# First expert of the second mixture: identity products in TensorE's waits, no zeroed output, Sinkhorn's sums in PSUM, one plain pair, another order of steps

## The chip, the cores and the metric

The kernel runs on one core of one Trainium2 chip, in fp32 throughout. The metric is device time in microseconds from launch to end, the median of three executions. TensorE runs at one of two granted clock levels, 1.2 or 2.4 GHz; a granted clock of 0.50 in a row is the lower one and 1.00 the upper. Engines are written here as TensorE (PE in the profile, PEld its weight loads), VectorE (DVE), ScalarE (ACT), GpSimd (POOL), and SP, which issues the DMAs.

## The reference

An attention stage (two kinds of softmax attention, added) gives `x` of 2304 tokens x 512. A soft mixture of 8 experts follows, and then the second mixture, in which the change lies:

```python
def _moe2_ref(x, w_gate, w1, w2):
    N, D = x.shape
    E = w_gate.shape[1]                       # 8 experts, D 512, F 1024, N 2304
    logits = x @ w_gate
    P = np.exp(logits - logits.max())
    for _ in range(8):                        # Sinkhorn
        P /= P.sum(1, keepdims=True) + 1e-09  # row sums
        P /= P.sum(0, keepdims=True) + 1e-09  # column sums
        P *= N / E
    out = np.zeros((N, D), dtype=np.float32)
    for e in range(E):
        h = np.maximum(x @ w1[e], 0.0)
        out += P[:, e:e + 1] * (h @ w2[e])
    return out
```

## The kernel before

The first mixture ends with a product `so` (L881) of eight experts' second weights, each half expert waiting for its own DMA of 1 MB. Its result goes through two copies (L888 on VectorE, L889 on ScalarE), a small product `sop` (L892) and a copy to `soT` (L895). x itself is never formed: `x = c @ slot_out`, so the second mixture folds `slot_out` into its first weights. `a_part` (L937 and the two engines' copies) and `a_sum` (L948, L952, L953) make this folded weight `a4s` for one half of an expert's 1024 hidden units.

The second mixture then takes 8 experts by 9 blocks of 256 tokens. In each block, `z_mm` (L1008) makes the hidden units z1 and z0 (two halves) in PSUM. ScalarE applies the ReLU and rounds to the fast matmul type (the high part, L1020, L1041), VectorE or GpSimd makes the low part (L1024, L1045), so that three fast products stand for one fp32 product. VectorE's `z_sum` (L1035) adds or subtracts quarters of h. The 2x2 product h @ w2 is computed by Strassen's scheme with seven products instead of eight: `product` (L1066, 12 matmuls each), from weight tiles `wt` whose high part ScalarE writes (`w_hi`, L991) and whose low part VectorE or GpSimd writes (`w_lo`, L998). Four of the weight tiles are sums of quarters of w2 (`w_sum`, L978, the tiles `ts`). The first block of the first expert is done plainly, with eight products (`plain`, L1079, 96 matmuls), since it needs no sums. Each block adds into `acc` by five updates (L1100, up_a to up_e), which VectorE reads from PSUM.

While the first expert runs, the gates are made beside it: `gate` (logits, their maximum, exp), then eight rounds of `sink`, each with row sums (L1182 to L1185), a matmul with ones for the column sums over partitions (L1189) and the column division (L1196 to L1200). A generator's step of these runs after each fifth product. The first expert adds without its gate, and is scaled by it later (L1143).

The order of all this is written by a table of numbers: each step is put on a plan `at(t, f, ...)`, where t is in units of one product, and the plan is sorted and issued. `P` holds the places of a block's steps, `W` those of the weight steps of experts 1 to 7 (with 0 or 1 for VectorE or GpSimd), `W0` and `P0` those of the first expert's weights and its plain block. Each engine does its own instructions in that order and waits at each for what it needs. PSUM has four buffers of one bank for y, ap, as, gl, gp and sp together, and two banks each for z1 and z0.

## Time and profile before

| what | us |
|---|---|
| median of 3 executions | 1060.66 (1058.97 to 1060.85) |
| the profiled execution, its own time | 1060.58 |
| its span, first to last instruction | 1058.9 |
| TensorE busy | 994.4 (94%) |
| VectorE busy | 744.3 (70%) |
| GpSimd busy | 642.8 (61%) |
| ScalarE busy | 546.2 (52%) |

So 1.7 us of the execution lie outside the span. Up to about 209 us the attention and the first mixture run. The first expert of the second mixture runs from there to about 361 us, and experts 1 to 7 to the end. Shares over the whole span hide that the stages differ, so the rows below are taken by stretch.

### The profile page before, as it was taken

The page shows a single profiled execution, that of the slowest core. Times are in us where ns is not written, and L with a number is a line of the kernel's source. Part 1 is how long each engine was busy: PE and PEld are TensorE (multiplying, and loading weights), DVE is VectorE, ACT ScalarE, POOL GpSimd, SP SyncE. Part 2 cuts the span into 40 slices and gives each one's busy share as a digit, 9 for nine tenths or more (in the row PEclk, how much of TensorE's full clock was granted, in tenths as well). Part 3 has the DMA queues.
Part 4 walks back from the last instruction along what each step waited for, and adds up shares of the span by engine and source line. Part 5 has one row for each costly group of instructions (what it writes and reads, how often), then busy time and mean ns, then how long its engine had stood idle before and what let it go on. Part 6 is the DMA issues. An engine that isn't in the chain of part 4 may idle for free.

```text
span 1058.9 us, 23713 instructions
## 1 busy us (share of the span) xinstructions
PE 994.4 (94%) x9663; PEld 919.1 (87%) x9663; DVE 744.3 (70%) x1264; ACT 546.2 (52%) x1032; POOL 642.8 (61%) x497
## 2 busy tenths in 40 slices
PE   6898888869887999999999999999999999999998
PEld 6777763249787989999999999999989999999998
DVE  4878762276889767686677767767767686677766
ACT  4666641143433655665555456545644564456543
POOL 5777552055355746784767486657746874768453
PEclk9999898869999999999999999999999999999999
DMA  9999999924001110130013001301120130000111
GB/s 192 175 187 238 261 312 391 387 79 157 1 1 41 60 62 2 41 120 1 1 41 120 2 2 39 120 1 41 53 68 2 41 98 23 2 2 21 40 61 61
DMA packets 86593, 93.89 MB, mean 89 GB/s; under 512 B 52052, under 2 KB 52052, under 8 KB 86484
## 3 DMA queue, kind: packets, MB, share of 16 engines
q1 hardware_dynamic: 86484, 92.37, 31.3%
q8 instruction: 77, 1.26, 0.6%
q14 instruction: 32, 0.26, 0.1%
HBM read 87.64 MB, written 4.72 MB: 87 GB/s over the span
## 4 chain that ended last, share of the span: by engine, by line
PE 55%; POOL 1%; DVE 0%; issue 0%
PE y L1066 49%; PE z L1008 5%; PE ap L937 1%; POOL wt L998 1%; PE as L948 0%; DVE acc L1100 0%
## 5 line engine op out<-in xcount | busy, mean ns | idle before, releaser
L1066 PE MATMUL y<-wt,ot 128*128 128x256 f32 x5964 | 770.0, 280 | 15.2 <-DVE acc L1100 9.5
L1066 PEld LDWEIGHTS y<-wt,ot 128*128 128x128 f32 x5964 | 737.1, 189 | 32.1 <-issue 19.4
L1045 POOL TENSOR_TENSOR ot<-ft,ot 128x512 fp32r<-128x512 f32 x284 | 379.1, 1356 | 296.8 <-ACT ot L1041 218.9
L1100 DVE SCALAR_TENSOR_TENSOR acc<-y,pg,acc 128x256 f32<-128x256 f32 x315 | 201.4, 639 | 186.1 <-PE y L1066 185.4
L1041 ACT ACTIVATE ot<-ft 128x512 fp32r<-128x512 f32 x284 | 172.4, 628 | 179.2 <-DVE ft L1035 179.1
L1020 ACT ACTIVATE ot<-z 128x512 fp32r<-128x512 f32 x217 | 129.3, 597 | 184.1 <-PE z L1008 149.8
L1035 DVE SCALAR_TENSOR_TENSOR ft<-z,ft 128x512 f32<-128x512 f32 x284 | 193.3, 681 | 0.2
L1008 PE MATMUL z<-c,a4s 128*128 128x256 f32 x576 | 160.7, 281 | 3.3 <-DVE ft L1035 2.4
L1024 DVE SCALAR_TENSOR_TENSOR ot<-z,ot 128x512 fp32r<-128x512 f32 x217 | 147.6, 681 | 0.0
L1008 PEld LDWEIGHTS z<-c,a4s 128*128 128x128 f32 x576 | 109.0, 190 | 4.6 <-DVE ft L1035 3.5
L1031 ACT ACTIVATE ft<-z 128x512 f32<-128x512 f32 x142 | 84.1, 592 | 0.0
L998 POOL TENSOR_TENSOR wt<-w2s,wt 128x1024 fp32r<-128x1024 f32 x16 | 38.6, 2410 | 10.0 <-ACT wt L991 10.0
L998 POOL TENSOR_TENSOR wt<-ts,wt 128x1024 fp32r<-128x1024 f32 x16 | 39.1, 2461 | 0.0
L509 POOL TENSOR_TENSOR pl<-pl,l 128x384 f32<-128x384 f32 x16 | 13.3, 832 | 40.5 <-DVE l L505 25.6
L520 DVE STREAM_TRANSPOSE bd<-pl 32x384 f32<-32x384 f32 x64 | 36.4, 569 | 1.4
L991 ACT ACTIVATE wt<-ts 128x1024 fp32r<-128x1024 f32 x32 | 33.6, 1054 | 6.6 <-DVE ts L978 3.3
L1100 DVE SCALAR_TENSOR_TENSOR acc<-y,acc 128x512 f32<-128x512 f32 (+1 forms) x44 | 24.6, 562 | 17.2 <-PE y L1066 11.9
L978 POOL TENSOR_TENSOR ts<-w2s 128x1024 f32<-128x1024 f32 x14 | 33.6, 2402 | 0.0
L399 ACT ACTIVATE kt<-knt 64x576 f32<-64x576 f32 x32 | 20.6, 644 | 14.1 <-DVE kd L391 13.8
L391 DVE TENSOR_REDUCE kd<-knt 128x144 f32<-128x576 f32 x16 | 12.1, 757 | 19.9 <-PE knt L341 13.7
L991 ACT ACTIVATE wt<-w2s 128x1024 fp32r<-128x1024 f32 x25 | 26.0, 1049 | 0.0
L998 DVE TENSOR_TENSOR wt<-ts,wt 128x1024 fp32r<-128x1024 f32 x16 | 25.1, 1568 | 0.0
(179 smaller groups left out, 852.2 us busy)
## 6 DMA issues: line engine op xcount, KB each, us to landing
wa<-in_moe_w_dram SPq DMA_DIRECT2D x32, 1024.0 KB, 12.6
w1s<-in_moe_w_dram SPq DMA_DIRECT2D x16, 1024.0 KB, 5.1
w2s<-in_moe_w_dram SPq DMA_DIRECT2D x16, 1024.0 KB
vw<-in_v_dram SPq DMA_DIRECT2D x62, 96.0 KB, 6.0
...
```

The lines of the kernel that those rows point to most:

```text
L520: nc.vector.transpose(out=bds[u % 2][32 * c:32 * c + 32, :, c, :], in_=U[u]["pl"][32 * c:32 * c + 32])
L991: nc.scalar.activation(out=tt[e, i][:, 0], in_=w_of(e, i), func=ACTF.Copy)
L998: eng.tensor_tensor(out=t[:, 1], in0=w_of(e, i), in1=t[:, 0].bitcast(FP32), op=ALU.subtract)
L1008: nc.tensor.matmul(out=zt[n, k][:, f, :], lhsT=a4s[e % 2][:, f0:f0 + 128], rhs=c4[:, BLK * b:BLK * b + BLK], start=True, stop=True,)
L1020: nc.scalar.activation(out=t[:, 0], in_=zv(n, i, k), func=ACTF.Relu)
L1024: nc.vector.scalar_tensor_tensor(out=t[:, 1], in0=zv(n, i, k), scalar=0.0, in1=t[:, 0].bitcast(FP32), op0=ALU.max, op1=ALU.subtract)
L1031: nc.scalar.activation(out=t, in_=zv(n, i, k), func=ACTF.Relu)
L1035: nc.vector.scalar_tensor_tensor(out=t, in0=zv(n, i, k), scalar=0.0, in1=ft[n, other], op0=ALU.max, op1=op)
L1041: nc.scalar.activation(out=t[:, 0], in_=ft[n, name], func=ACTF.Copy)
L1045: nc.gpsimd.tensor_tensor(out=t[:, 1], in0=ft[n, name], in1=t[:, 0].bitcast(FP32), op=ALU.subtract)
L1066: nc.tensor.matmul(out=yt[n, bank][:, HD * half:HD * half + HD], lhsT=ot[n, name][:, l, f, :], rhs=tt[e, j][:, r, f, :], start=(m == 0 and ...
L1100: nc.vector.scalar_tensor_tensor(out=o, in0=in_, scalar=pg[:, t, e:e + 1] if e else 1.0, in1=o, op0=ALU.mult, op1=ALU.add)
```

## The change

Six edits, all but the last in the first expert or just before it:

1. `fill(n)` issues n identity products (128x128 times 128x128, into a PSUM tile that nothing reads): 9 before each half of the last two experts' `so`, 3 before `sop`, 4 after it, 4 after the first `a_part` and 4 after the first `a_sum`.
2. `acc` is no longer zeroed by GpSimd (five memsets, L1296). The first update of each part of `acc` is a copy. `CP = (1, 0)`: for the first 128 tokens of a block it is done by ScalarE, for the second by VectorE. `up_b` of the first expert becomes a ScalarE copy of one half and a VectorE addition of the other.
3. Sinkhorn's row sums and column sums lie in the PSUM tile `sp` instead of SBUF, taken at the start of a round instead of at its matmul, and the last two instructions (divide, times N/E) become one.
4. `gate_part`'s copy of `soT` (L1217) goes from VectorE to ScalarE.
5. The first expert's weights are loaded in the order w1 half 1, w2 half 1, w1 half 0, w2 half 0, and the second `a_part`/`a_sum` are steps of the plan.
6. New tables: `P1` for the first expert's blocks (P stays for the others), and new numbers in `P0`, `W0` and `W`.

```diff
+P1 = {'z1': 5.13,
+ 'z0': 3.41,
...
+CP = (1, 0)
+FILL = (9, 3, 4, 4, 4)
...
- '6l': (67.58, 1),
- 'ld1': 9.4,
- 'ld2': 9.71}
+ '6l': (67.81, 0),
+ 'ld1': 2.33,
+ 'ld2': 16.73}
...
+        idle = ps.tile([128, 512], FP32, name="idle", tag="idle", bufs=1)
+
+        def fill(n):
+            for _ in range(n):
+                nc.tensor.matmul(out=idle[:, 0:128], lhsT=ident, rhs=ident, start=True, stop=True)
...
+                if e >= E - 2 and j % 4 == 0:
+                    fill(FILL[0])
                 nc.tensor.matmul(
                     out=so[32 * g:32 * g + 32, :], lhsT=hT[:, j, e, :], rhs=w[:, j % 4, :],
...
-        if not e:
-            need(("zero", t // 4))
         o = acc[:, t, :] if out_ is None else acc[:, t, HD * out_:HD * out_ + HD]
         if in_.shape != o.shape:
             o = o.rearrange("p (h d) -> p h d", h=2)
+        if first and not e:
+            if CP[i]:
+                nc.scalar.activation(out=o, in_=in_, func=ACTF.Copy)
+            else:
+                nc.vector.tensor_copy(out=o, in_=in_)
+            return
         nc.vector.scalar_tensor_tensor(
...
     def up_b(n):
-        update(n, 0, None, yt[n, 0])
+        if n < NB:
+            update(n, 0, 1, yt[n, 0][:, HD:], True)
+            update(n, 0, 0, yt[n, 0][:, 0:HD])
+        else:
+            update(n, 0, None, yt[n, 0])
...
     def sink():
-        nc.vector.tensor_reduce(out=rs[:, :, 0], in_=pg, axis=AX.X, op=ALU.add)
+        sp = yt.tile("sp", [128, DM], FP32, "sp", "y")
+        rs = sp[:, 160:160 + NT]
+        cs = sp[:, 192:192 + E]
+        nc.vector.tensor_reduce(out=rs, in_=pg, axis=AX.X, op=ALU.add)
         nc.vector.tensor_scalar(out=rs, in0=rs, scalar1=EPS, scalar2=None, op0=ALU.add)
         nc.vector.reciprocal(out=rs, in_=rs)
...
-        nc.vector.tensor_tensor(out=pg, in0=pg, in1=cs_.to_broadcast([128, NT, E]), op=ALU.mult)
-        nc.vector.tensor_scalar(out=pg, in0=pg, scalar1=float(N) / E, scalar2=None, op0=ALU.mult)
+        nc.vector.scalar_tensor_tensor(
+            out=pg, in0=pg, scalar=float(N) / E,
+            in1=cs.rearrange("p (o e) -> p o e", o=1).to_broadcast([128, NT, E]), op0=ALU.mult, op1=ALU.mult,
+        )
...
-    for i in range(2):
+    for i in (1, 0):
         load_w1(0, i)
-    for i in (1, 0):
         load_w2(0, i)
...
+    a_part(0, 1)
+    fill(FILL[3])
+    a_sum(0, 1)
+    fill(FILL[4])
...
-        nc.vector.tensor_copy(out=so4, in_=soT.to_broadcast([128, KD, 4, NS]))
+        nc.scalar.activation(out=so4, in_=soT.to_broadcast([128, KD, 4, NS]), func=ACTF.Copy)
```

Three places where the order moves. The first is TensorE from the last half expert of `so` to the first products of the plain block; before, its rows are these (ap, as: the folded weight of one half; z1, z0: hidden units; y: products):

```order
L881 MATMUL so_2898<-wa_2843,hT_2882 32x512 x4
L892 MATMUL sop_3007<-stack_70,hs_2884 128x32 x4
L937 MATMUL ap_3064<-w1s_3050,soT_77 32x512 x4
L937 MATMUL ap_3072<-w1s_3048,soT_77 32x512 x4
L948 MATMUL as_3080<-aps_3069,a4s_3024 128x512 x2
L948 MATMUL as_3085<-aps_3077,a4s_3024 128x512 x2
L1008 MATMUL z1_3098<-c4_2885,a4s_3024 128x256 x4
L1008 MATMUL z0_3106<-c4_2885,a4s_3024 128x256 x4
L1079 MATMUL y_3120<-wt_3057,ot_3103 128x256 x12
```

And after (idle: the identity products):

```order
L842 MATMUL idle_2762<-ident_69 128x128 x9
L924 MATMUL so_2899<-wa_2844,hT_2883 32x512 x4
L842 MATMUL idle_2762<-ident_69 128x128 x3
L936 MATMUL sop_3047<-stack_70,hs_2885 128x32 x4
L842 MATMUL idle_2762<-ident_69 128x128 x4
L982 MATMUL ap_3107<-w1s_3090,soT_77 32x512 x4
L1272 MATMUL idle_3106<-ident_69 128x128 x4
L993 MATMUL as_3119<-aps_3112,a4s_3068 128x512 x2
L1272 MATMUL idle_3106<-ident_69 128x128 x4
L982 MATMUL ap_3133<-w1s_3094,soT_77 32x512 x4
L1053 MATMUL z1_3142<-c4_2886,a4s_3068 128x256 x4
L993 MATMUL as_3151<-aps_3138,a4s_3068 128x512 x2
```

The second half's `a_part` and `a_sum` stand behind the first half's, around z1, and the identity products fill the places between.

The second is VectorE in the first expert's third and fourth blocks, where one round of Sinkhorn ends and the next begins (pg: the gates; rs, cs: row and column sums). Before:

```order
L953 TENSOR_TENSOR a4s_3024<-as_3640,a4s_3024 64x512
L1196 TENSOR_REDUCE cs_3047<-sp_3625 128x8
L1197 TENSOR_SCALAR cs_3047<-cs_3047 128x8
L1198 RECIPROCAL cs_3047<-cs_3047 128x8
L1199 TENSOR_TENSOR pg_76<-pg_76,cs_3047 128x144
L1200 TENSOR_SCALAR pg_76<-pg_76 128x144
L1100 SCALAR_TENSOR_TENSOR acc_3023<-y_3623,acc_3023 128x256
L1182 TENSOR_REDUCE rs_3046<-pg_76 128x18
L1183 TENSOR_SCALAR rs_3046<-rs_3046 128x18
L1184 RECIPROCAL rs_3046<-rs_3046 128x18
L1185 TENSOR_TENSOR pg_76<-pg_76,rs_3046 128x144
```

And after, at the same round:

```order
L998 TENSOR_TENSOR a4s_3068<-as_3682,a4s_3068 64x512
L1250 TENSOR_REDUCE sp_3611<-sp_3611 128x8
L1253 TENSOR_SCALAR sp_3611<-sp_3611 128x8
L1254 RECIPROCAL sp_3611<-sp_3611 128x8
L1255 SCALAR_TENSOR_TENSOR pg_76<-pg_76,sp_3611 128x144
L998 TENSOR_TENSOR a4s_3068<-as_3724,a4s_3068 64x512
L1236 TENSOR_REDUCE sp_3736<-pg_76 128x18
L1237 TENSOR_SCALAR sp_3736<-sp_3736 128x18
L1238 RECIPROCAL sp_3736<-sp_3736 128x18
L1239 TENSOR_TENSOR pg_76<-pg_76,sp_3736 128x144
L1149 SCALAR_TENSOR_TENSOR acc_3067<-y_3666,acc_3067 128x256
```

Every instruction of a round now has an operand in the PSUM tile sp, L1200 is gone, and the update of acc that stood between the two rounds stands behind both.

The third is GpSimd in the first expert's weights (ts: sums of w2's quarters, wt: low parts). Before:

```order
L1296 MEMSET acc_3023 128x2048
L998 TENSOR_TENSOR wt_3063<-w2s_3052,wt_3063 128x1024
L978 TENSOR_TENSOR ts_3093<-ts_3093,w2s_3052 128x1024
L978 TENSOR_TENSOR ts_3128<-w2s_3052,ts_3093 128x1024
L1296 MEMSET acc_3023 128x2048
L998 TENSOR_TENSOR wt_3056<-w2s_3054,wt_3056 128x1024
L1296 MEMSET acc_3023 128x2048
L998 TENSOR_TENSOR wt_3059<-ts_3128,wt_3059 128x1024
```

And after:

```order
L1023 TENSOR_TENSOR ts_3128<-ts_3128,w2s_3092 128x1024
L1043 TENSOR_TENSOR wt_3105<-w2s_3092,wt_3105 128x1024
L1023 TENSOR_TENSOR ts_3223<-w2s_3092,ts_3128 128x1024
L1043 TENSOR_TENSOR wt_3098<-w2s_3096,wt_3098 128x1024
L1043 TENSOR_TENSOR wt_3101<-ts_3223,wt_3101 128x1024
L1043 TENSOR_TENSOR wt_3102<-ts_3128,wt_3102 128x1024
```

The memsets are gone, and the second sum (`ts`) stands ahead of the first low part.

## Rows read from the trace of the kernel before

**Rows 1.** The page's first part: busy us, share, instructions of each engine.

```profile
PE 994.4 (94%) x9663; PEld 919.1 (87%) x9663; DVE 744.3 (70%) x1264; ACT 546.2 (52%) x1032; POOL 642.8 (61%) x497
```

**Rows 2.** TensorE's waits, 207 to 360 us, then (last row) from 360: us, times, longest.

```profile
PE y L1066 <- DVE acc L1100: 9.5, 5, 3.9
PE z L1008 <- DVE ft L1035: 2.4, 2, 1.6
...
PE y L1066 <- POOL wt L998: 3.8, 4, 1.2
```

**Rows 3.** Stretches: length, busy of PE, PEld, DVE, ACT, POOL, granted clock, DMA, GB/s.

```profile
252.60:364.70 112.10, 98.35 (x774) 93.47 (x774) 95.75 (x177) 48.49 (x82) 56.24 (x38) 0.95 0.03 11
...
206.00:208.00 2.00, 1.23 (x12) 0.20 (x8) 0.00 (x0) 0.00 (x0) 0.00 (x0) 0.50 1.05 388
```

**Rows 4.** TensorE's instructions by line, 252.6 to 364.7 us: count, busy, mean ns, idle before.

```profile
L1066 PE MATMUL y<-wt,ot 128*128 128x256 f32 x671 | 94.3, 289 | 11.1 <-DVE acc L1100 9.5 <-DVE ot L1024 1.5
L1008 PE MATMUL z<-c,a4s 128*128 128x256 f32 x64 | 18.6, 291 | 2.6 <-DVE ft L1035 2.4
```

**Rows 5.** TensorE's timeline in a later expert: start, us, instructions.

```profile
515.21 6.06 PE L1066 MATMUL y<-wt,ot 128*128 128x256 f32 x52
521.11 0.28 PE L1008 MATMUL z<-c,a4s 128*128 128x256 f32 x1
```

**Rows 6.** VectorE's instructions by line, 252.6 to 364.7 us.

```profile
L1100 DVE SCALAR_TENSOR_TENSOR acc<-y,acc 128x512 f32<-128x512 f32 (+1 forms) x39 | 22.6, 580 | 11.9 <-PE y L1066 11.8
...
L1199 DVE TENSOR_TENSOR pg<-pg,cs 128x144 f32<-128x144 f32 x8 | 8.6, 1069 | 0.3
L1200 DVE TENSOR_SCALAR pg<-pg 128x144 f32<-128x144 f32 x8 | 6.7, 834 | 0.3
L1185 DVE TENSOR_TENSOR pg<-pg,rs 128x144 f32<-128x144 f32 x8 | 5.0, 621 | 0.3
L1183 DVE TENSOR_SCALAR rs<-rs 128x18 f32<-128x18 f32 x8 | 4.8, 600 | 0.3
```

**Rows 7.** Timeline of VectorE and GpSimd around 280 us.

```profile
277.52 0.69 DVE L953 TENSOR_TENSOR a4s<-as,a4s 64x512 fp32r<-64x512 f32 x1
279.82 2.17 DVE L1199 TENSOR_TENSOR pg<-pg,cs 128x144 f32<-128x144 f32 x1
...
279.48 2.35 POOL L978 TENSOR_TENSOR ts<-w2s 128x1024 f32<-128x1024 f32 x1
```

**Rows 8.** TensorE's timeline from the last experts of `so` to the second block.

```profile
200.47 1.06 PE L881 MATMUL so<-wa,hT 128*32 128x512 f32 x8
207.66 1.93 PE L881 MATMUL so<-wa,hT 128*32 128x512 f32 x8 [0.78 <-DMA wa<-in_moe_w_dram]
210.24 1.89 PE L892 MATMUL sop<-stack,hs 128*128 128x32 f32 x8 [0.64 <-DVE hs L888]
...
213.18 3.64 PE L937 MATMUL ap<-w1s,soT 128*32 128x512 f32 x16 [1.05 <-DMA w1s<-in_moe_w_dram]
219.38 1.62 PE L1008 MATMUL z<-c,a4s 128*128 128x256 f32 x8 [0.54 <-DVE a4s L953]
225.76 4.61 PE L1079 MATMUL y<-wt,ot 128*128 128x256 f32 x26 [2.31 <-DVE ot L1024]
232.89 1.06 PE L1220 MATMUL gp<-wg_sb,so 128*128 128x8 f32 x8 [2.52 <-DVE so L1217]
...
247.07 0.62 PE L1066 MATMUL y<-wt,ot 128*128 128x256 f32 x4
```

**Rows 9.** Weight loads around one Sinkhorn product (two passes of 144 columns).

```profile
263.62 0.30 PEld L1189 LDWEIGHTS sp<-pg,a4s 128*128 128x128 f32 x2
263.85 0.89 PEld L1066 LDWEIGHTS y<-wt,ot 128*128 128x128 f32 x7
```

**Rows 10.** VectorE's timeline: the copy for the gates' product.

```profile
229.69 3.15 DVE L1217 COPY so<-soT 128x512 f32<-128x512 f32 x1
```

**Rows 11.** Low parts of weights on VectorE, whole span: ns min/median/max.

```profile
L998 DVE TENSOR_TENSOR wt<-ts,wt x16: 1226/1346/2867, 236.5 to 965.2; 128x1024 fp32r<-128x1024 f32 x16
```

More of the change, by code (lines that the diff above doesn't have):

```diff
@@ L77 @@
  'ue': 7.47}
-NPLAIN = 1
-P0 = ((-3.45, -3.16, -2.01, 1.77, -1.6, 2.91, -0.95, 0.59, 5.1, 6.1, 8.71, 8.08),
- (-1.58, 2.82, -3.83, -10.07, -3.18, 3.82, 1.07, -4.42, 1.7, 2.01, 10.07, 9.98))
-W0 = {'0h': -9.21,
- '6h': -6.84,
- '1h': -4.85,
- '7h': -0.9,
- '2h': 2.44,
- '3h': 2.25,
- '4h': 3.75,
- '5h': 4.98,
- 'gp': 2.21,
- 'g': 4.46,
- '0l': (-8.05, 0),
- '6l': (-5.5, 1),
- '1l': (-2.28, 0),
- '7l': (1.08, 1),
- 't1': (-7.68, 0),
- 't2': (-0.28, 1),
- 't4': (0.56, 1),
- 't3': (3.48, 0),
- '2l': (2.5, 1),
- '3l': (5.33, 0),
- '4l': (4.74, 0),
- '5l': (5.44, 1)}
-W = {'ap': 14.61,
- 'as': 19.65,
- 't1': (22.65, 1),
- 't2': (33.72, 1),
- 't4': (38.68, 1),
- 't3': (40.91, 1),
- '0h': 44.89,
- '1h': 41.33,
- '2h': 57.7,
- '3h': 59.91,
- '4h': 56.58,
- '5h': 61.69,
- '6h': 66.19,
- '0l': (48.68, 1),
- '1l': (45.62, 0),
- '2l': (59.61, 1),
- '3l': (62.44, 1),
- '4l': (59.48, 0),
- '5l': (65.8, 0),
- '6l': (67.58, 1),
- 'ld1': 9.4,
- 'ld2': 9.71}
+P1 = {'z1': 5.13,
+ 'z0': 3.41,
+ 'a12h': -3.58,
+ 'a12l': -1.99,
+ 'h22': -4.08,
+ 'a11h': -1.57,
+ 's1': -1.49,
+ 'h11': -2.05,
+ 'a11l': -1.4,
+ 'a22h': -0.77,
+ 's2': -1.31,
+ 'a22l': -0.67,
+ 's2h': 0.14,
+ 's2l': 0.89,
+ 's4': -0.35,
+ 's1h': -0.3,
+ 's3': 0.49,
+ 's1l': 0.04,
+ 's3h': 2.53,
+ 's3l': 3.57,
+ 's4h': 2.73,
+ 's4l': 4.29,
+ 'ua': 2.0,
+ 'ub': 4.76,
+ 'ud': 5.16,
+ 'uc': 5.93,
+ 'ue': 7.23}
+NPLAIN = 1
+CP = (1, 0)
+FILL = (9, 3, 4, 4, 4)
+P0 = ((-4.08, -3.79, -3.03, 0.91, -0.28, 3.53, 1.09, 1.8, 6.07, 7.22, 7.12, 10.0),
+ (-4.0, 6.94, -19.64, -11.36, 2.38, -1.13, 12.86, -14.23, 7.99, -0.51, 3.32, 12.21))
+W0 = {'ap': -8.9,
+ 'as': -3.41,
+ '0h': -12.47,
+ '6h': -10.55,
+ '1h': -3.76,
+ '7h': 2.78,
+ '2h': 3.51,
+ '3h': 5.6,
+ '4h': 6.66,
+ '5h': 5.66,
+ 'gp': 2.2,
+ 'g': 3.57,
+ '0l': (-9.11, 0),
+ '6l': (-3.19, 1),
+ '1l': (-2.75, 0),
+ '7l': (3.45, 1),
+ 't1': (-24.54, 0),
+ 't2': (-5.8, 1),
+ 't4': (3.1, 1),
+ 't3': (4.64, 0),
+ '2l': (5.77, 1),
+ '3l': (6.91, 1),
+ '4l': (8.5, 0),
+ '5l': (7.12, 0)}
+W = {'ap': 14.93,
+ 'as': 21.66,
+ 't1': (27.31, 1),
+ 't2': (34.27, 1),
+ 't4': (38.09, 1),
+ 't3': (41.61, 1),
+ '0h': 50.43,
+ '1h': 42.64,
+ '2h': 56.78,
+ '3h': 59.79,
+ '4h': 56.6,
+ '5h': 61.35,
+ '6h': 65.61,
+ '0l': (53.1, 0),
+ '1l': (48.5, 1),
+ '2l': (60.79, 1),
+ '3l': (61.41, 1),
+ '4l': (59.9, 0),
+ '5l': (66.97, 0),
+ '6l': (67.81, 0),
+ 'ld1': 2.33,
+ 'ld2': 16.73}
 class Ring:
@@ L1146, in attn_moe_moe_kernel @@
     nc.gpsimd.memset(ones, 1.0)
-    rs = mm.tile([128, NT, 1], FP32, name="rs")
-    cs_ = mm.tile([128, 1, E], FP32, name="cs")
     def gate():
@@ L1209, in attn_moe_moe_kernel, with fill @@
         tt.tile((0, i), [128, 2, HF, HD], FP32R, "wt", "t")
-    for i in (1, 0):
-        a_part(0, i)
-    for i in (1, 0):
-        a_sum(0, i)
+    zt.tile("idle", [128, HF, BLK], FP32, "idle", "z0")
+    def fill(n):
+        for _ in range(n):
+            nc.tensor.matmul(out=zt["idle"][:, 0, 0:128], lhsT=ident, rhs=ident, start=True, stop=True)
+    a_part(0, 1)
+    fill(FILL[3])
+    a_sum(0, 1)
+    fill(FILL[4])
     def gate_part():
         so4 = ft.tile("so4", [128, KD, 4, NS], FP32, "so4", "f")
-        nc.vector.tensor_copy(out=so4, in_=soT.to_broadcast([128, KD, 4, NS]))
+        nc.scalar.activation(out=so4, in_=soT.to_broadcast([128, KD, 4, NS]), func=ACTF.Copy)
         gp = yt.tile("gp", [128, E], FP32, "gp", "y")
@@ L1290, in attn_moe_moe_kernel @@
         ):
-            at(t0 + P[name], f, n, *args)
+            at(t0 + (P if e else P1)[name], f, n, *args)
         if e == 1:
@@ L1294, in attn_moe_moe_kernel @@
                 at(t0 + 0.6 + i, mul_p0, n, i)
-    def zero(i):
-        nc.gpsimd.memset(acc[:, 4 * i:min(4 * i + 4, NT), :], 0.0)
-        made.add(("zero", i))
-    zero(0)
-    for i in range(1, -(-NT // 4)):
-        at(i, zero, i)
     V, G = nc.vector, nc.gpsimd
     at(W0["gp"], gate_part)
+    at(W0["ap"], a_part, 0, 0)
+    at(W0["as"], a_sum, 0, 0)
     at(W0["g"], g_copy)
```

33 lines of the change are left out of this document (19 added, 14 removed).

## The prediction

> **What bounds the kernel now.** The page says that TensorE is busy for 94% of the span [rows 1], so the first question is where the other 6% lie. I asked who TensorE waits for, in two stretches [rows 2]. From 360 us on there are only four waits of about 1 us, 3.8 us in all, for GpSimd's low part of a weight tile. Nearly all the rest lies in the first expert, 207 to 360 us, and there the name that comes back is VectorE: 9.5 us in five waits for an update of acc, one of them 3.9 us long, and 2.4 us for a z_sum. The later experts run at TensorE's pace; the first one does not.
>
> So I took the first expert alone: 252.6 to 364.7 us, from the second block to the first update of the second expert, 112.1 us [rows 3]. TensorE is called busy for 98.35 us there, but "busy" holds half-clock time and modelled ends, so I count work instead. The trace has 671 products and 64 z matmuls [rows 4]. One costs, where nothing waits and the clock is at the upper level, 5.90 us / 52 = 0.1135 us (521.11 - 515.21) [rows 5]. 735 of them are 83.4 us. The rest of the stretch's matmuls (16 passes of Sinkhorn's products, two a_part, two a_sum and three small ones) I put at 6 us: 16 passes at about 0.115 make 1.8 and the others some 4. TensorE's own work is thus 89.4 us, and 22.7 of the 112.1 us are not work. They are waits of 13.7 us (11.1 + 2.6, the idle times of rows 4), and half-clock time after them: the mean granted clock is 0.95 [rows 3], 5% of 112 us or 5.6 us; some 3 us I cannot place.
>
> Why VectorE is late is read in two steps. It is busy for 95.75 of the 112.1 us [rows 3], and part of that is no work [rows 6]: the four Sinkhorn lines L1199, L1200, L1185 and L1183 take 25.1 us for 32 instructions on at most 144 elements. The timeline shows what they do [rows 7]: L1199 starts at 279.82 and takes 2.17 us, to 281.99, and GpSimd's w_sum runs from 279.48 to 281.83. It ends when GpSimd's instruction ends. L953 at 277.52, with one operand in PSUM, takes its usual 0.69 us. So an all-SBUF instruction of these forms waits for GpSimd's running instruction, and VectorE does its work in order, so the updates and z_sums behind it wait too, and then TensorE.
>
> The Trainium skill (SBUF — State Buffer, the section on engine and DMA ports) has the rule: VectorE and GpSimd share one port pair under an exclusive lock, taken by a VectorE instruction with two SBUF inputs or in a two-port mode, and the loser stands still for the whole instruction. Rows 7 agree. By it the sums in PSUM lift the lock altogether, but a weight's low part moved to VectorE, with two SBUF inputs, goes under it; that is weighed below as a term.
>
> **Blocks two to nine of the first expert.** An undisturbed one of them lies between 0.19 us (L953's 0.69 [rows 7] scaled from 512 to 144 elements) and 0.69; I take 0.31 for 144 elements, which is 2.5 for eight, and 0.18 for the 18 elements of L1183, 1.4 for eight. The excess is 8.6 - 2.5, 5.0 - 2.5, 4.8 - 1.4, and L1200 goes whole with 6.7: 18.7 us less for VectorE. The first update of each 128 tokens becomes a copy; for the first 128 tokens ScalarE does it, one 256-wide and half of a 512-wide update per block. Rows 6 give 22.6 us for 39 updates, five per block; a quarter of their elements go, about 5 us over the stretch. ScalarE takes them beside its 48.49 of 112.1 us [rows 3], which hides them. VectorE then has 95.75 - 18.7 - 5 = 72 us to do in a stretch of 89.4: it is no longer the slower one, and TensorE's waits for it should nearly go. What is late next is VectorE at an unlucky order (a round's eight instructions, some 2 us, in front of an update). I leave 3 of the 22.7 us: gain 19.7. Ends: 22.7 (all of it goes) and 10 (13 us of waits stay, since an engine that is 80% busy in a fixed order can still be late).
>
> **From `so` to the second block.** The identity products first. The trace shows none; the nearest row is a Sinkhorn product of two fp32 passes, whose first weight load starts at 263.62 with the next instruction's at 263.85: 0.23 us [rows 9]. I take 0.23 for one, nine cost 2.1 us. Ends: half (one pass, 0.12), and double at the half clock. Before, half an expert of `so` starts at 200.47 and takes 1.06 us, and the last starts at 207.66, when its DMA has landed, and takes 1.93 at the half clock [rows 8], which is 0.50 at 206 to 208 us [rows 3]. After: four times 2.1 + 1.06 from 200.47 is 213.0, against 207.66 + 1.93 = 209.6. The fillers are longer than the waits that they fill, and `so` ends 3.4 us later. With half the price it ends at 209.6 or before.
>
> That is given back behind it. Before, z starts at 219.38, 9.8 us after `so` [rows 8]. At the upper clock sop's 1.89 halves (0.9 less), the DMA wait of 1.05 is over by then, and the chain holds one a_part of about 1.06 in front of its sum instead of two at 3.64 (2.6 less), but the second half's a_part in front of z (up to 1.1 more). 9.8 - 0.9 - 1.05 - 2.6 + 1.0 = 6.2, so z at 219.2: as before. The fills of 3 and 4 stand in front of products that wait for copies anyway.
>
> Then come the weights. Before, steady products begin at 225.76 [rows 8]; w_sum and low parts share the port there, one operation at a time. After, it is the same chain with w2's half 1 landed earlier: if VectorE gets the port for its first low part ahead of GpSimd's sum I reach 225.0, if GpSimd is first about 2.3 us later (its 2.35 us, rows 7): 225.0 to 227.3. From there to the second block: 96 products and 8 z at 0.1135 are 11.8, gp 1.06 [rows 8], and a half-clock start like that of before, where 26 products took 4.61 us instead of 2.95: 1.7. Together 14.6, so the second block begins at 239.6 to 241.9, against 247.07 [rows 8]. The waits of before between are 2.52 us for VectorE's L1217 [rows 8], which took 3.15 us [rows 10] and goes to ScalarE, others for the memsets' port and the half clock they led to; what hides the copy is that ScalarE has it done before 27 products are through. If that cover fails, gp waits again, 2.5 us. Gain 5.2 to 7.5, I take 6.3. Ends: -3.4 (the later `so` is passed on whole and nothing is won) and 9.
>
> **Experts 1 to 7.** Their blocks keep table P; W moves weight steps. One matters: the low part of tile 6, which the four waits of rows 2 were for, goes from GpSimd, where it stood behind four low parts of products, to VectorE, where a low part takes 1.35 us in the middle and 2.87 at most [rows 11]. It stands between two updates, and GpSimd's queue loses one operation. Gain 1.5, ends 3.8 (all four waits go) and -8: seven experts with 2.87 - 1.35 us each on the path are -10.6, less what of the waits goes. w1 of the next expert is loaded earlier and w2 later, each some 10 products, 10 x 12 x 0.1135 = 13.6 us, ahead of its first use: nothing.
>
> By the skill's lock rule alone the moved low part meets GpSimd's operations, as rows 11's maximum shows; the sum would be 1.5 us higher than mine.
>
> **Sum**, against the profiled execution's 1060.6 us, which is the median to 0.1: 1060.6 - 19.7 - 6.3 - 1.5 = 1033.1. All low ends: 1060.6 - 22.7 - 9 - 3.8 = 1025. All high ends: 1060.6 - 10 + 3.4 + 8 = 1062, but they are of different mechanisms and hardly meet.
>
> **Rivals.**
> (a) The lock stays: pg still lies in SBUF as input and output, and one operand in PSUM might not be enough. Then L1200 goes (6.7) and 5 us of updates, of 23.7 us on VectorE: about half of the gain, 10 us, 1060.6 - 10 - 6.3 - 1.5 = 1043. For it: nothing of just this form is in the trace. Against: L953 ran beside GpSimd at 0.69 [rows 7].
> (b) The fillers cost what they take: `so`'s 3.4 us later is passed on and the second block begins 3 us later than before instead of 6.3 earlier: 1033.1 + 9.7 = 1043. For it: 13.0 > 9.6 by the price of rows 9. Against: the a_parts and sop behind run at the half clock now [rows 8].
> (c) Slower: the sums hold a PSUM buffer. sp is held for 8 of a round's 13 steps, from the row sums to the last division, in place of 2; with eight rounds in about 90 us that is 7 us in place of 1.7; four buffers serve y, ap, as and sp. If a product's bank then comes free only at the division, TensorE stands once a round; at the longest wait of rows 2, 3.9 us, eight rounds cost 31 us and the time is 1033.1 + 31 = 1064. It decides from 27.5 us on, 3.4 us a round. Against: a block needs two buffers, and the two of the block before are free by its third product.
> (d) No change: the gain meets a new wait of the same size. TensorE would have to find 27 us of waits in 130 us again; I see no queue for that.
>
> **Chances.** My forecast 0.70 (its own range 1026 to 1040), (a) 0.11, (b) 0.11, (d) 0.03, (c) 0.05. The range of 8 in 10 takes the forecast with (a) and (b), with some room above: 1025 to 1046. A measurement of this kernel tells 0.2% (2.1 us) from no change. Faster 0.92, same 0.03, slower 0.05.
>
> **What would show it.** In the changed profile: the Sinkhorn instructions each at 0.2 to 0.35 us with none near 1 us or above (else (a)); VectorE near 72 us in the first expert's blocks and TensorE's waits for acc under 3 us; `so` ending near 213 us with the granted clock at 1.00 (earlier shows the fillers cheaper); the second block at 240 to 242 us (250 is (b)); the second expert's first update near 338 us instead of 364.7; and no more than 4 us of waits behind it. Long waits of TensorE ended by the division of a round, L1255, are (c). Wrong I would be most likely in what I leave for waits in the first expert, since VectorE's order there is all new.

## The result, and the profile after

The changed kernel takes 1024.2 us (median of four runs, 1023.0 to 1025.1) against 1059.8 for the kernel before (four runs beside it, 1058.6 to 1060.9): ratio 0.9664, 95% interval 0.9647 to 0.9681. The forecast was 1033.1 with a range of 1025 to 1046: the direction was right, the time 8.9 us under the forecast and 0.8 us under the range. The profiled execution is one of 1024.1 us, span 1022.4, so the spans differ by 36.5 us. Disturbed runs are left out of all totals here and below.

I cut both traces at three points: the start of the last cp product in `so`, the weight load of the first gl product (in the second block) and the second expert's first update. "Way" is from the first to the second, "blocks 2 to 9" to the third, "behind" from there to the last product's start. "Slow" counts, behind the first expert, the steps from one matmul's start to the next of 115.5 to 120 ns; why is told below.

| us | last cp | way | blocks 2 to 9 | behind | slow |
|---|---|---|---|---|---|
| before | 200.3 | 47.1 | 117.3 | 690.4 | 2286 |
| changed | 201.8 | 40.4 | 95.5 | 681.0 | 669 |
| gain | -1.5 | 6.7 | 21.8 | 9.4 | |

The page's engine line, which answers to [rows 1]: TensorE is busy 96%.

```profile
PE 982.9 (96%) x9765; PEld 914.2 (89%) x9765; DVE 726.4 (71%) x1252; ACT 552.8 (54%) x1051; POOL 618.4 (60%) x485
```

Blocks 2 to 9 as one stretch (length, busy of PE, PEld, DVE, ACT, POOL, granted clock), to be read against [rows 3], and VectorE's lines in it against [rows 6]:

```profile
242.15:337.65 95.50, 95.50 (x821) 93.22 (x820) 76.92 (x170) 55.33 (x102) 60.85 (x41) 1.00 0.11 37
```

```profile
L1149 DVE SCALAR_TENSOR_TENSOR acc<-y,acc 128x256 f32<-128x256 f32 (+1 forms) x24 | 12.1, 505 | 5.5 <-ACT acc L1145 5.5
L1147 DVE COPY acc<-y 128x512 f32<-128x512 f32 (+1 forms) x10 | 6.3, 634 | 2.1 <-PE y L1111 2.1
...
L1239 DVE TENSOR_TENSOR pg<-pg,sp 128x144 f32<-128x144 f32 x8 | 2.4, 304 | 0.3
L1255 DVE SCALAR_TENSOR_TENSOR pg<-pg,sp 128x144 f32<-128x144 f32 x8 | 2.4, 304 | 0.3
...
L1237 DVE TENSOR_SCALAR sp<-sp 128x18 f32<-128x18 f32 x8 | 1.5, 184 | 0.3
L1253 DVE TENSOR_SCALAR sp<-sp 128x8 f32<-128x8 f32 x8 | 1.4, 174 | 0.3
```

TensorE is busy for all of it at the full clock, and its list of waits is empty there. The Sinkhorn lines that took 0.60 to 1.07 us each take 0.17 to 0.30. Behind the first expert TensorE waits 3.7 us in all, no longer for GpSimd's wt [rows 2] but in seven short waits for an update:

```profile
PE y L1111 <- DVE acc L1149: 3.7, 7, 0.6
```

The low part that W moved to VectorE stands in front of such an update: at 439.46 us, for one, it takes 2.25 us, and TensorE waits 0.59 us for the update behind it.

TensorE's timeline from `so` to the second block, against [rows 8]:

```profile
201.89 2.17 PE L842 MATMUL idle<-ident 128*128 128x128 f32 x18
203.99 1.06 PE L924 MATMUL so<-wa,hT 128*32 128x512 f32 x8
...
213.59 1.07 PE L924 MATMUL so<-wa,hT 128*32 128x512 f32 x8
...
217.25 1.06 PE L982 MATMUL ap<-w1s,soT 128*32 128x512 f32 x8
...
226.84 1.09 PE L1053 MATMUL z<-c,a4s 128*128 128x256 f32 x4 [1.41 <-DVE a4s L998]
227.73 4.56 PE L1124 MATMUL y<-wt,ot 128*128 128x256 f32 x27
232.13 0.95 PE L1284 MATMUL gp<-wg_sb,so 128*128 128x8 f32 x8
```

`so` ends at 214.7, 12.8 us behind the start of what follows the last cp (9.1 before), in halves of 1.06 at the upper clock; nine identity products are 18 rows of the trace (two matmuls each) in 2.10 us, 0.233 for one product, as priced. In all there are 51 identity products, 36 of them inside `so`; they are the 102 matmuls that the changed kernel has more.

**Where the 9.4 us behind the first expert come from.** The waits of before there were 3.8 us. What else is gone shows only when products are counted. Three windows of 20 us in before (length, TensorE's busy time and instructions, granted clock, DMA):

```profile
520.00:540.00 20.00, 20.00 (x179) 1.00 0.15 54
620.00:640.00 20.00, 20.00 (x172) 1.00 0.17 54
...
820.00:840.00 20.00, 20.00 (x172) 1.00 0.16 54
```

The same kind of steps, busy for 100% at the same granted clock, and 172 matmuls instead of 179. In the timeline of before the slow kind is

```profile
614.82 6.29 PE L1066 MATMUL y<-wt,ot 128*128 128x256 f32 x52
620.94 0.28 PE L1008 MATMUL z<-c,a4s 128*128 128x256 f32 x1
```

6.12 us for 52, 117.7 ns each, where [rows 5] has 113.5. Step by step the trace has two paces, 113.3 and 117.8 ns, and TensorE keeps one for up to 592 steps. Before ran 2286 of its 5878 steps slow, three experts nearly whole (601 to 671, 800 to 870, 901 to 971 us); after 669, none for more than 42 in a row. 1617 steps of 4.5 ns are 7.2 us. The other 2.2 lie in the steps of over 120 ns, 106 before and 96 after; the listed waits hold almost nothing of it (3.8 and 3.7 us).

### The profile page after: what moved, and what is told of

It is laid out like the page before. It is cut to its first block, busy times and chain, and to the rows that moved or that the text cites. A ratio compares the mean times of both kernels' runs of the same rounds, so it can differ in the third digit from the quotient of the medians.

```text
span 1022.4 us, 23912 instructions
## 1 busy us (share of the span) xinstructions
PE 982.9 (96%) x9765; PEld 914.2 (89%) x9765; DVE 726.4 (71%) x1252; ACT 552.8 (54%) x1051; POOL 618.4 (60%) x485
## 4 chain that ended last, share of the span: by engine, by line
PE 86%; DMA 5%; DVE 5%; ACT 2%; SPq 1%; issue 1%; POOL 1%; DVEq 0%; ACTq 0%; POOLq 0%
PE y L1111 65%; PE z L1053 6%; DMA kn<-in_k_dram 2%; DMA vw<-in_v_dram 2%; DVE wt L1043 2%; PE h L871 2%; PE so L924 1%; PE ap L982 1%; PE y L1124 1%; PE idle L842 1%; DVE acc L1149 1%; DMA wa<-in_moe_w_dram 1%; PE qnt L368 1%; PE knt L368 1%; PE as L993 1%
## 5 line engine op out<-in xcount | busy, mean ns | idle before, releaser
L1111 PE MATMUL y<-wt,ot 128*128 128x256 f32 x5964 | 754.0, 277 | 3.7 <-DVE acc L1149 3.7
L1111 PEld LDWEIGHTS y<-wt,ot 128*128 128x128 f32 x5964 | 725.3, 188 | 12.5 <-issue 9.9
L1043 DVE TENSOR_TENSOR wt<-w2s,wt 128x1024 fp32r<-128x1024 f32 x16 | 30.4, 1902 | 8.0 <-ACT wt L1036 7.9
L1023 POOL TENSOR_TENSOR ts<-ts,w2s 128x1024 f32<-128x1024 f32 x8 | 20.1, 2508 | 20.5 <-DVE ts L1023 20.5
L987 DVE TENSOR_TENSOR aps<-ap,aps 128x512 fp32r<-128x512 f32 x16 | 11.1, 691 | 23.6 <-ACT aps L986 23.6
```

What stands on the lines that cost most here:

```text
L1023: eng.tensor_tensor(out=tsum(e, name), in0=a, in1=b, op=op)
L1043: eng.tensor_tensor(out=t[:, 1], in0=w_of(e, i), in1=t[:, 0].bitcast(FP32), op=ALU.subtract)
L1111: nc.tensor.matmul(out=yt[n, bank][:, HD * half:HD * half + HD], lhsT=ot[n, name][:, l, f, :], rhs=tt[e, j][:, r, f, :], start=(m == 0 and ...
```

## The experiments

All totals are medians, with the range of the runs; the kernel before ran beside each group with medians of 1059.6 to 1061.2 us and single runs from 1054 to 1070. The stages come from one profile of each kernel; the last cp starts anywhere between 198.2 and 207.5 us in them, which no edit of mine touches, so I go by stages.

| kernel | way | blocks 2 to 9 | behind | slow | total us (range) |
|---|---|---|---|---|---|
| before_again | 47.5 | 118.8 | 689.3 | 2072 | 1062.4 (one run) |
| before_new_w | 45.9 | 115.9 | 680.1 | 575 | 1050.2 (1046.9 to 1053.4) |
| before_nudge | 44.1 | 117.5 | 694.2 | 3341 | 1067.9 (1065.9 to 1070.3) |
| before_gap | 47.3 | 117.5 | 685.4 | 830 | 1055.4 (1053.4 to 1059.3) |
| before_a4s | 45.1 | 118.5 | 684.3 | 383 | 1055.2 (1053.2 to 1058.3) |
| before_psum_sums | 42.0 | 100.1 | 692.5 | 2806 | 1042.9 (1040.9 to 1043.5) |
| after_again | 40.3 | 95.5 | 680.1 | 480 | 1022.5 (1019.6 to 1026.8) |
| after_third | 40.4 | 95.5 | 680.7 | 597 | 1023.5 (1022.6 to 1025.3) |
| after_old_w | 40.2 | 96.9 | 684.1 | 858 | 1026.8 (1024.4 to 1029.5) |
| after_gap | 40.6 | 95.7 | 684.3 | 1507 | 1025.5 (1023.4 to 1030.2) |
| after_a4s | 40.7 | 97.3 | 698.4 | 5722 | 1043.7 (1043.1 to 1045.7) |
| after_sbuf_sums | 40.3 | 103.0 | 680.3 | 511 | 1030.1 (1028.0 to 1030.9) |
| after_old_order | 40.5 | 99.5 | 681.1 | 629 | 1026.5 (1024.8 to 1027.3) |
| after_no_fill | 39.7 | 95.5 | 680.5 | 545 | 1020.8 (1019.9 to 1024.5) |
| after_late_fills | 37.0 | 95.5 | 680.6 | 584 | 1021.4 (1018.1 to 1022.1) |
| best | 40.9 | 95.5 | 681.2 | 719 | 1021.4 (1019.8 to 1022.7) |
| best2 | 32.0 | 95.6 | 681.0 | 681 | 1019.1 (1017.6 to 1020.9) |

**The pace: is it the program's, and what moves it?** before_again is before unchanged.

> The kernel before once more, with a profile. In the first profile TensorE's products keep one of two paces behind the first expert, 113.3 ns or 117.8 ns from start to start, and hold it over up to 592 products: 2286 slow ones behind the first expert in before, 669 in after, which at 4.5 ns each is 7.2 of the 9.4 us that experts 1 to 7 gained. Theory A (the program sets the pace: how each wait or odd product falls decides it, and it falls the same in each execution): the same stretches are slow again (570 to 583, 601 to 670, 770 to 782, 800 to 870, 901 to 971 us), 2286 slow products give or take 150, time 1058 to 1061 us. Theory B (the pace is drawn anew in each execution): other stretches are slow, the count moves by several hundred, and the time with it by 2.7 us for each stretch of 592.

Neither theory whole. The count is 214 lower, which is more than theory A allows, and of the three long stretches two come again. The windows of its profile:

```profile
520.00:540.00 20.00, 20.00 (x172) 1.00 0.04 6
620.00:640.00 20.00, 20.00 (x172) 1.00 0.04 4
...
920.00:940.00 20.00, 20.00 (x178) 1.00 0.01 2
```

Again three experts are slow, two of them the same as before (606 to 675 and 805 to 874 us) and one another (505 to 575 us in place of 901 to 971): the program alone does not fix the pace.

before_nudge adds an odd product in each later expert (shortened):

```diff
+        if m == 0 and j == 0 and e and b == 4:
+            nc.tensor.matmul(out=yt[n, bank][:, 0:32], lhsT=ot[n, name][:, 0, 0, :],
+                rhs=tt[e, j][:, 0, 0, 0:32], start=True, stop=True, skip_group_check=True)
```

> The kernel before with one more product of 32 columns ahead of the first product of the fifth block of each of experts 1 to 7; the product behind it overwrites what it writes. It costs seven times 0 to 0.23 us by itself. Theory A (the pace is a state of TensorE's own stream, held until something odd comes by): the pace changes at some of the seven places, most of all in the stretches that are slow for 592 products, and from there the stretch runs at the other pace; where all three turn fast the time falls by up to 3 times 590 times 4.5 ns = 8 us (1052 us), where fast ones turn slow it grows by 2.7 us each. Theory B (the slow pace comes from what lies or runs beside the products in those experts: addresses, ports, other engines): slow and fast stretches stay where they were, time 1060 to 1061.5 us.

```profile
409.97 3.00 PE L1071 MATMUL y<-wt,ot 128*128 128x256 f32 x25
412.81 0.18 PE L1064 MATMUL y<-wt,ot 128*128 128x32 f32 x1
412.83 3.43 PE L1071 MATMUL y<-wt,ot 128*128 128x256 f32 x27
416.10 0.28 PE L1008 MATMUL z<-c,a4s 128*128 128x256 f32 x1
```

Theory A: the pace is a state of TensorE's own stream. Up to the odd product 25 products take 2.84 us, 113.6 ns each; then come steps of 27 and 201 ns, and from there on 117.8. Five of the seven experts turn from fast to slow there, a sixth was slow already, and they stay so for up to 540 steps; in the other (513 us) a slow stretch turns fast. The time grows by 8 us, where I had thought mainly of the other direction; the products themselves cost about 0.8 us.

before_new_w and after_old_w exchange the table W (here some of the lines that differ):

```diff
- '1h': 41.33, '0h': 44.89, 'ld1': 9.4, 'ld2': 9.71, '6l': (67.58, 1),
+ '1h': 42.64, '0h': 50.43, 'ld1': 2.33, 'ld2': 16.73, '6l': (67.81, 0),
```

> The kernel before with one part of the change: the new table W, which places the loads, the A sums and the weight halves of experts 1 to 7. Theory A (W moves the waits behind which the slow pace begins): the time from the second expert's first update to the end falls from 694.2 us to 685 to 688, the slow products from 2286 to under 1000, total 1050 to 1054 us. Theory B (what the end of the first expert leaves over, loads and buffers, gave the 9.4 us): 1059 to 1061 us. Theory C (W takes waits away, and the pace has no part in it): 1057 to 1058 us, with the 2.2 us of waits and the slow products as many as before.

> The changed kernel with the old table W for experts 1 to 7. Theory A (W decides the stretches at the slow pace): 1030 to 1034 us, 1500 to 2400 slow products behind the first expert. Theory B (the first expert's end gave the 9.4 us): 1023 to 1026 us. Theory C (waits alone): 1026 to 1027 us.

Putting W into before brings all of it, 10.3 us behind the first expert, with 575 slow steps: theory A. Taking it out of the changed kernel costs only 3.1, with 858: theory C. Something else in the change ends slow stretches too. In the changed kernel 41 of its 43 slow stretches end at a z product; in before the seven stretches of over 100 steps ran through 188 z products and ended at an a_part or at a longer step (some 300 ns); the long ones of before_new_w, up to 114 steps, end at an a_part or an a_sum. The sums' two SBUF tiles are gone from the pool ahead of ot, so the products' weights lie 128 bytes lower: the program's allocation has ot at 182944 before and 182816 after, which is 160 and 32 modulo 256, and the z products' weights a4s at 160 in both. This side effect of the third edit stands in no list of the change. Two kernels shift ot by 128 bytes (with ft behind it, which the products do not read):

```diff
-    mm.tile([128, 24], FP32, name="gap")
+    mm.tile([128, 56], FP32, name="gap")
```

> The kernel before with nothing changed but an unused strip of SBUF that is 128 bytes a partition longer, so that the tiles ot and ft (the products' weights) lie 128 bytes further on, at an address that is 32 modulo 256 as in the changed kernel, not 160 as before; no instruction moves. In the traces so far a slow stretch (117.8 ns a product) ends at a z product after 11 to 40 products where ot lies at 32, and runs on to the next wait, up to 592 products, where it lies at 160, as the z products' weights do. Theory A (the address decides whether a z product ends the slow pace): slow products behind the first expert fall from 2286 and 2072 to under 1100, no stretch over 120; time 1049 to 1054 us. Theory B (something else of the change ends them: the PSUM banks of z0 and z1 that are swapped, the order in the first expert): as before, 1054 to 1062 us with stretches of 592 slow ones.

> The changed kernel with the same strip 128 bytes longer, so that ot lies at 160 modulo 256 as in the kernel before. Theory A (address): a slow stretch that begins behind a wait lasts to the next wait. There is such a start behind the A sums of each of the seven experts, so with each that is drawn slow 570 products more run at the slow pace, 2.6 us each: slow products behind the first expert from 669 to 1200 to 4700, time 1027 to 1042 us. If none is drawn slow, the short slow stretches of 13 to 38 products still no longer end at a z product. Theory B: 1023 to 1026 us, 669 slow products give or take 150.

Theory A in both by the stretches: none over 42 steps is left in the one, and in the other 738 steps at the end and stretches of 168 and 114 run slow. The totals fit it less: 1055.4 us lies above theory A's 1054, though before_gap is clear of before (ratio 0.9954, 0.9927 to 0.9981), and 1025.5 below its 1027. Then a4s alone was shifted:

```diff
-    a4s = [a4[:, 80:80 + F], a4[:, 80 + F:80 + 2 * F]]
+    a4s = [a4[:, 112:112 + F], a4[:, 112 + F:112 + 2 * F]]
```

> The changed kernel with the z products' weights a4s 128 bytes further on in their tile, at 32 modulo 256 as ot is (before the shift 160); no instruction moves. Theory A (the difference between the two kinds of weights ends a slow stretch): slow stretches run on to the next wait as in the kernel before, at least three of over 100 products behind the first expert, 1000 slow products or more, from the second expert's first update to the end 682.5 us or longer. Theory B (the address of ot alone, 32 against 160): 480 to 850 slow products, no stretch over 90, 680 to 682 us.

> The kernel before with a4s 128 bytes further on, at 32 modulo 256, ot staying at 160. Theory A (the difference): no stretch of over 120 slow products behind the first expert, under 1100 in all, from the second expert's first update to the end 684 to 687 us, total 1053 to 1057 us. Theory B (the address of ot alone): stretches of 592 again in some experts, 1200 to 4000 slow products, 687 to 697 us.

Theory A in both: the address of ot alone does not decide it, that of a4s counts as well. The same shift that makes before faster by 0.5% (ratio 0.9953, 0.9935 to 0.9971) costs the changed kernel some 20 us with no instruction moved. Its windows have 172 or 173 matmuls all through, and no wait ends it (the first row is the changed kernel's, to compare):

```profile
420.00:440.00 20.00, 20.00 (x179) 1.00 0.18 58
...
420.00:440.00 20.00, 20.00 (x172) 1.00 0.04 4
520.00:540.00 20.00, 20.00 (x172) 1.00 0.00 1
620.00:640.00 20.00, 20.00 (x173) 1.00 0.00 1
```

So with ot and a4s at 160 and 160 both paces hold until something odd comes by; at 32 and 160, or 160 and 32, a slow stretch mostly ends at a z product (the longest has 51 steps) and the fast pace stays; at 32 and 32 only the slow one holds, in one kernel. Equal addresses do not behave alike, so the difference is not the whole rule either. Why is not shown, and no other pair was tried.

**The lock and the order in the first expert.** after_sbuf_sums puts the sums back (shortened; the fused multiplication stays):

```diff
-        sp = yt.tile("sp", [128, DM], FP32, "sp", "y")
-        rs = sp[:, 160:160 + NT]
-        cs = sp[:, 192:192 + E]
+        rs, cs = rs_, cs_          # tiles of the pool mm; sp is taken ahead of its product
```

> The changed kernel with the Sinkhorn sums rs and cs back in SBUF tiles (the address of ot modulo 256 kept at 32; the fused multiplication of L1255 kept). Theory A (the lock of VectorE against GpSimd is what the first expert's excess was): the instructions at L1237 to L1240 and L1253 to L1255 that work on SBUF alone take up to 1 to 2 us again beside GpSimd's, VectorE falls behind, TensorE waits for acc; of the 22.7 us of excess that went in blocks 2 to 9, 8 to 20 us come back: 1032 to 1044 us. Theory B (the new order P1 and the missing zeroing made the room, the lock did not matter): 1024 to 1027 us.

Its stretch of blocks 2 to 9, and the lines that answer to L1239, L1253, L1255 and L1237 of the changed kernel:

```profile
240.94:343.95 103.01, 98.34 (x821) 95.12 (x820) 89.95 (x170) 55.45 (x102) 60.30 (x41) 0.98 0.11 35
```

```profile
L1240 DVE TENSOR_TENSOR pg<-pg,rs 128x144 f32<-128x144 f32 x8 | 9.8, 1227 | 0.3
...
L1254 DVE TENSOR_SCALAR cs<-cs 128x8 f32<-128x8 f32 x8 | 4.7, 589 | 0.3
...
L1256 DVE SCALAR_TENSOR_TENSOR pg<-pg,cs 128x144 f32<-128x144 f32 x8 | 3.6, 450 | 0.3
L1238 DVE TENSOR_SCALAR rs<-rs 128x18 f32<-128x18 f32 x8 | 3.2, 394 | 0.3
```

The four lines take 21.3 us instead of 7.7, VectorE is busy 89.95 instead of 76.92, and TensorE waits again (3.6 us for acc, 1.0 for ft): 7.5 us, just under theory A's 8. Its total of 1030.1 lies between the theories. before_psum_sums is the other direction, the changed `sink` in before with ot's address kept:

> The kernel before with the Sinkhorn alone as in the change: its sums in a PSUM tile, the factor fused into the last multiplication; the address of ot is kept at 160 modulo 256. Putting the sums back into SBUF cost the changed kernel 7.5 us of 95.5 in its first expert. Theory A (the lock is the main part of the 22 us that the stretch of blocks 2 to 9 lost): VectorE's busy time there falls from 96 to about 78 us, TensorE's waits for acc and ft by more than half, the stretch from 117.3 to 101 to 107 us, total 1046 to 1053 us. Theory B (the lock is a third, the order of the steps and the zeroed output the rest): VectorE's time falls as much, but the stretch only to 108 to 113 us, total 1051 to 1057 us. Theory C (the PSUM tile, now held through the reductions, keeps a y buffer from the products): TensorE's waits end at L1255's counterpart, stretch 116 us or longer.

```profile
245.35:345.50 100.15, 97.40 (x821) 93.55 (x820) 79.48 (x175) 50.17 (x85) 59.88 (x40) 1.00 0.10 33
```

Better than theory A: 17.2 us of the stretch, total 0.982 of before (0.9789 to 0.985), though the total also holds a way that is 5.1 us shorter in its profile. No wait at the division: rival (c) does not occur. Two things changed at once here, the sums' place and the fused multiplication; the trace of before says which weighs more. Of the 32 instructions of L1183, L1185, L1199 and L1200, 16 started beside a running GpSimd instruction: each ended 0.03 to 0.17 us behind that one and took 0.74 to 2.17 us. The other 16 took 0.18 to 0.31 us. In before_psum_sums 20 of the 32 like them (L1185, L1187, L1201, L1203) started beside one, and none took over 0.31. L1200 alone takes 0.23 us, so of its 6.7 us 1.9 are work that the fusion saves, and the rest is such standing still. after_old_order gives blocks 2 to 9 the table P again:

```diff
-            pz = P if e else P1
+            pz = P if n else P1
...
-            at(t0 + (P if e else P1)[name], f, n, *args)
+            at(t0 + P[name], f, n, *args)
```

> The changed kernel with the old table P for blocks 2 to 9 of the first expert in place of P1 (the z products of the plain block stay as they are). Theory A (with the lock gone the order decides nothing): stretch of blocks 2 to 9 95.5 to 97.5 us, total within 2 us of the changed kernel. Theory B (P1 is what took the waits for acc and ft): TensorE waits 5 to 14 us again in the stretch, 101 to 110 us, total 1029 to 1038 us.

99.5 us, between the two: the waits are 1.8 us (1.1 for ScalarE's first copy of acc). So the 21.8 us are 17.2 for Sinkhorn's edit, mostly the lock, and 4.0 for P1; 0.6 is left for the rest. Back in the changed kernel the lock costs only 7.5: there the fused instruction stays, and 12 of 32 instructions are held up, against 20 of 40 in before (with L1197). What the new order adds to that was not taken apart.

**The identity products.** after_no_fill sets FILL to (0, 0, 0, 0, 0), after_late_fills to (0, 3, 4, 4, 4).

> The changed kernel with none of the 102 identity products. Theory A (they keep TensorE's clock at full rate through so, sop, ap and as): without them these steps run at the half clock again, as in before, where so to the first block's products took 12.4 us from the end of so instead of the 13.1 to 14 now but each product half as fast; the clock falls to 0.5 from the last so products on and stays low into the first products y: 6 to 8 us longer, 1030 to 1032 us. Theory B (they cost what they save; 102 times 0.11 us is 11 us, part of it in time that was idle): 1021 to 1025 us.

> The changed kernel without the 72 identity products inside so (FILL[0] is 0), but with the 30 behind so. Without any, the way from the last cp to the second block was 39.7 us against 40.4, and it ran at the half clock from 203.0 to 226.9 us; the identity products inside so made so 4.1 us longer and those behind it went with a stretch that was 2.3 to 3.5 us shorter. Theory A (once the clock has fallen inside so, 30 products do not bring it back in time): clock 0.50 to about 225 us, the way 40 to 42 us. Theory B (they do): clock 1.00 from sop or ap on, so as short as without fills, the way 36 to 38.5 us, and total 2 to 4 us under the changed kernel.

(The 102, 72 and 30 in these texts are matmuls, two for each of 51, 36 and 15 products.) Without any, the way is 0.7 us shorter, not 6 to 8 longer, and the total of 1020.8 lies at the edge of theory B, though its clock is at 0.50 (203 to 226 us, first row) where that of the changed kernel is at 1.00 (second fence):

```profile
203.00:226.00 23.00, 16.92 (x63) 7.86 (x64) 9.63 (x11) 8.51 (x14) 7.18 (x3) 0.50 0.57 210
```

```profile
203.00:226.00 23.00, 20.77 (x158) 13.82 (x156) 6.48 (x10) 5.92 (x10) 2.85 (x1) 1.00 0.67 247
```

What the full clock wins behind `so`, the 36 products inside `so` cost ahead of it. With them `so` ends 12.9 us behind the last cp's start in each of eight profiles, without them 9.9 here; from there to the second block it is 27.5 us with all identity products and 29.7 without any. With the late ones alone the way is 37.0, inside theory B's range, and the total only 1.0 us under the changed kernel beside it, not 2 to 4. Its clock was 1.00 through `so` up to 222 us, so this execution does not tell whether they bring back a clock that has fallen. One wait is uncovered, for the aps that stands on VectorE behind t1, which waits 2.5 us for its transfer:

```profile
222.87 0.80 PE L993 MATMUL as<-aps,a4s 128*128 128x512 f32 x1 [3.44 <-DVE aps L987]
```

best and best2 move what stood ahead of it (gathered from FILL and the table W0, the old values first):

```diff
-FILL = (9, 3, 4, 4, 4)      't1': (-24.54, 0)   't2': (-5.8, 1)   '0l': (-9.11, 0)
+FILL = (0, 3, 4, 4, 4)      't1': (-8.8, 0)                       '0l': (-8.7, 0)     (best)
+FILL = (0, 3, 4, 4, 4)      't1': (-3.38, 0)    't2': (-3.1, 1)   '0l': (-3.6, 0)     (best2)
```

> The changed kernel without the identity products inside so, and with t1 (L1023) and 0l (L1043) moved on VectorE behind the second aps (L987): there t1 waited 2.5 us for the transfer of w2s with aps, as and z queued behind it, and TensorE waited 3.4 us for that aps. Theory A (that wait goes whole): the way from the last cp to the second block from 37.0 to 33.5 to 35 us, total 1016 to 1020 us. Theory B (what is moved back is needed at once: 0l and t1's sums now hold back the z_lo of the plain block and POOL's t2): 36.5 to 38.5 us, total 1020 to 1024 us.

> The changed kernel without the identity products inside so, with t1 (L1023) on VectorE behind the second a4s (L998), 0l (L1043) directly ahead of that a4s, and t2 on GpSimd behind 6l. Theory A (what is left of the way is TensorE's own work and the chain ap, aps, as, a4s, z): the wait for a4s falls from 3.1 to 1 to 2.2 us, the way from the last cp to the second block is 33.5 to 38 us, by whether the clock falls inside so, against 40.2 to 40.9; total 2 to 6 us under the changed kernel beside it. Theory B (0l, now behind z_lo, or t1's sums become late for the first products y): new waits of y for wt of 2 us and more, the way 39 to 42 us, total within 2 us of the changed kernel.

For best the total is theory B's, the way of 40.9 above both: z now waits 3.1 us for a4s behind t1 and 0l (first row), and the clock fell inside `so` at 203.6 us. It was back at 213.9, with the late identity products running, where after_no_fill stayed at 0.50 to 226.9. best2 has the way at 32.0, under the range, its wait for a4s being 2.5 us instead of 1 to 2.2 (the other rows). Part of that is luck: the last cp came late in this execution (203.6 us), so that `so` waited 0.2 us for wa instead of 3.1 in best, and the clock never fell. From the end of `so` to the second block it is 27.7 us, against 27.5 in the changed kernel, 30.5 in after_late_fills and 31.7 in best:

```profile
224.00 1.14 PE L1053 MATMUL z<-c,a4s 128*128 128x256 f32 x4 [3.10 <-DVE a4s L998]
...
217.42 0.50 PE L993 MATMUL as<-aps,a4s 128*128 128x512 f32 x1 [0.23 <-DVE aps L987]
220.41 0.74 PE L1053 MATMUL z<-c,a4s 128*128 128x256 f32 x4 [2.49 <-DVE a4s L998]
220.99 3.34 PE L1124 MATMUL y<-wt,ot 128*128 128x256 f32 x27
```

best2 is faster than both kernels: 1019.1 us against 1023.5 for the changed one beside it, ranges apart, and 0.9614 of before (0.9590 to 0.9638).

> The changed kernel once more, beside the others. Theory A (with ot at 32 modulo 256 no slow stretch lasts): 500 to 850 slow products behind the first expert, the way from the second expert's first update to the end 680 to 682 us, total 1022 to 1027 us. Theory B (its first execution was lucky): stretches of some 570 slow products in some of the seven experts, 2.6 us each.

> The changed kernel once more, timed beside best2. Both theories: the way from the last cp to the second block 40.2 to 40.6 us, 1020 to 1026 us.

Both executions of the changed kernel repeat its three stages within 0.9 us, with 480 and 597 slow steps and none for more than 47 in a row.

## Why the prediction was right or wrong

- **The step that failed: "Experts 1 to 7. Gain 1.5, ends 3.8 and -8."** It measured 9.4, outside both ends. The term counted waits and put the time of the products themselves at no change. The waits came out at nearly nothing: the four for GpSimd's wt went, as forecast, but seven for an update behind the moved low part came (3.8 us before, 3.7 after). What it left out is the pace. Its one price of a product, 0.1135 us, came from a block that happened to run at the fast pace [rows 5]; 2286 steps of before ran at 117.8 ns, busy at the full clock, so that no list of waits showed them, and 1617 fewer of these are 7.2 of the 9.4 us. W alone ends nearly all of the long slow stretches (before_new_w), and so does the new address of ot alone (before_gap); why either does is not shown, and together they bring the gain once. My end of -8 for the low part of tile 6 on VectorE did not come. The profiled execution lies 9.0 us under the sum of 1033.1: 7.9 of them are this term, 2.1 blocks 2 to 9, -1.0 the way.
- **Blocks 2 to 9, gain 19.7:** 21.8. The excess went as worked out, down to the single instruction; I had left 3 us for waits, and there are none. VectorE is at 76.92 us against the 72 worked out. Rival (a) is refuted by L1239 and L1255, which run at 0.30 us with pg in SBUF.
- **`so` to the second block, gain 6.3:** 5.3 by the time axis, 6.7 from the last cp. The number was right, its reason was not, so that it fits is luck. I had the identity products pay by the clock; as a whole they cost 0.7 us. `so` ended 3.7 us later, as worked out (3.4); against the execution without them they cost 3.0 us there and gave 2.2 back behind it. Rival (b) is right in its premise and wrong in its time: what shortened the way by 7.4 us without them is the rest of the change there (one a_part ahead of its sum, the copy so4 on ScalarE, no memsets), which I did not take apart.
- **"Before" is not one number on the way either:** 42.0 to 47.5 us over seven profiles with that code there. The spread lies ahead of the end of `so`, 4.7 to 9.9 us behind the last cp's start, by how long `so` still waits for wa (0.6 us in the shortest, 3.7 in the longest); from there on it is 37.3 to 38.8. The 47.1 that I started from was near the upper end, and against their median of 45.9 the changed kernel's 40.4 is 5.5 shorter.
- **The lock:** as the prediction had it. With the sums in SBUF an instruction on 8 elements (L1254) takes 0.589 us, with them in PSUM (L1253) 0.174, and of the 20 in before_psum_sums that ran beside GpSimd none was held up. The Trainium skill (SBUF — State Buffer, the section Who interferes with whom) says that a VectorE instruction with at most one SBUF input, outside the two-port modes, does not contend with GpSimd, and that TENSOR_SCALAR can enter such a mode. The traces agree with both, by these numbers.
